# Six groups instead of eight in the first phase of a two-layer network, and register reads queued behind weight loads

## The chip, the core and the metric

The kernel runs on one core of a Trainium2 chip. A core has a matrix engine (TensorE, PE in the profile), a vector engine (VectorE, DVE), an activation engine (ScalarE, ACT), a general engine (GpSimd, POOL) and a queue engine (SyncE, SP), which issues most of the DMAs. Each works through its own instructions in order, and they wait for each other by semaphores. The metric is device time in microseconds, lower is better; the median of three runs is shown.

## The reference

Three blocks follow each other, all in float32.

```python
# attention with rotary embedding: 2 batches, 8 heads, 576 tokens, 64 wide
scores = scale * matmul(rotate(q), rotate(k).T); attn = softmax(scores); x = attn @ v   # -> 1152 tokens x 512
# first network: 512 -> 2048 -> 512
h = x @ w_in
g = maximum(h, 0) + log1p(exp(-abs(h)))          # softplus
x = g @ w_out
# second network: each token with x @ w_skip > 0 goes to the best of 8 experts, 512 -> 1024 -> 512
e_idx = argmax(xc @ w_gate); gate_w = softmax(...)[e_idx]
out[do_compute] = xc + gate_w * (maximum(xc @ w1[e], 0) @ w2[e])
```

`w_in` and `w_out` are scaled so that float32 accuracy is needed; the weights of the first network arrive as 64-bit words.

## The kernel before

Every product of float32 data is made from halves: a tile is split into a high part, which ACT writes, and the rest, which DVE writes, and three matmuls (high by high, low by high, high by low) take the place of one.

**Attention** fills the first 184 us. It ends with `xh` and `xl`, the two halves of its output, in the layout in which the first network reads them.

**First network** (class `Moe1`). The 2048 hidden units are 16 groups `f` of 128. `weights(f)` loads a group's rows of `w_in` and `w_out` through SP (two loads into a staging ring `st` of two buffers) and unpacks them: on DVE three integer instructions (L561 to L563), on ACT a copy (L565), on DVE a subtraction (L566), for each of the two halves. `hidden(ci, f)` multiplies a range `ci` of tokens (L579) and computes softplus with six instructions of ACT and four of DVE per range (twice for a range of two blocks). `out_mm` (L620) adds the group's share to the output tiles, which stay in PSUM. PSUM holds five output tiles beside the rest, so the work goes in phases, `ranges` in the main function: phase 0 takes the first 512 tokens with groups 0 to 7, phase 1 the other 640 tokens with all 16 groups, phases 2 and 3 the first and second 256 of the first 512 tokens with groups 8 to 15. What phase 0 added up is kept in `part` and added again at the end of phases 2 and 3. Groups 8 to 15 therefore stay in SBUF from phase 1 to the end: `ring` says which pool a group's buffer comes from, `ahead` in which step `(phase, f)` it is asked for. The out matmuls of a step are written two steps behind its hidden ones (`pend`, `second`).

**Routing** runs beside phases 2 and 3: as soon as an output tile is ready it is written to `x2d`, transposed and multiplied with the gate (`turned`, `logits`), and `route` works out the place of its tokens. `first_tile` and `fetch(0)` gather the first 128 tokens of expert 0 early. `EARLY` names the steps in which the first five chunks of that expert's weights are loaded (through the same staging ring) and split (`split_w`), `XGT` the step in which the gathered rows are transposed. The last steps and the first tile's hidden matmuls are written in a fixed order (`REST`, `MORE`).

**Second network** (class `Moe2`, method `tiles`). Sorted by expert, the tokens are up to 17 tiles of 128 rows, 9 here. A tile needs eight chunks of weights of 128 x 1024, four of `w1` (part 0) and four of `w2` (part 1), each loaded into its buffer `raw[c]` by SP and split by ACT (L842) and DVE (L846). The expert of tile `T` and whether it differs from the one before are read by SP from the tensor `ei` into registers (`next_w`, L941 and L942); a load whose tile has the expert of the tile before is issued but moves nothing. `nt`, the number of tiles, is read by all engines for the `If` behind the ninth tile (L1220).

**Order.** Except for the part written by hand, a planner sets each engine's order from the order of the program and a simulated timeline of its own: an instruction that it believes ready may be put ahead of others of the same engine. `issue_after(x)` makes what is traced inside it follow `x` on `x`'s engine; it adds no wait.

Of the kernel before, what the change touches and what calls it, by code (L numbers as in the profile page):

```python
# [38 lines left out]
EARLY_RAW = 1  # L39
LATE_W = 4  # L40
HOLD = ((3, 15),)
EARLY = ((2, 11), (2, 12), (2, 13), (3, 10), (3, 12))
XGT = (3, 13)
REST = ((12, 13), (14,))

# [580 lines left out]
class Moe2:  # L626
# [4 lines left out]
    def __init__(self, tc, w_skip, w_gate, w1, w2, cst, x2d, out, rp, sp):  # L631
        self.tc, self.nc = tc, tc.nc
        nc = tc.nc
        self.w1, self.w2, self.cst, self.x2d, self.out, self.rp, self.sp = w1, w2, cst, x2d, out, rp, sp
        self.w9 = rp.tile([128, 4, 9], F32, name="w9")
        nc.scalar.dma_start(self.w9[:, :, 0:8], w_gate.rearrange("(k p) e -> p k e", p=128))
        with nc.allow_non_contiguous_dma(reason="512 words once"):
            nc.scalar.dma_start(self.w9[:, :, 8:9], w_skip.rearrange("(k p o) -> p k o", p=128, o=1))
        self.found_rows, self.late = None, (None, None)
        self.oh = rp.tile([128, 9, 8], BF16, name="oh")  # L640
        self.routed = []
        self.tok = rp.tile([128, 9, 1], F32, name="tok")
        self.xg, self.did = {}, {}
        self.lg = rp.tile([128, 9, 9], F32, name="lg")
        self.m0 = rp.tile([128, 9], F16, name="m0")
        self.extra = None
        self.ohp = sp.tile([128, 9, 128], F16, name="ohp")
        self.at = sp.tile([128, 9, self.ST], F32, name="at")
# [170 lines left out]
    def load_chunk(self, r, e, c, queue=None, **kw):  # L819
        queue = queue or self.nc.sync  # L820
        es = slice(e, e + 1) if isinstance(e, int) else bass.ds(e, 1)
        if c < 4:
            queue.dma_start(r, self.w1[es, 128 * c : 128 * c + 128, :].rearrange("o p n -> p (o n)"), **kw)
        else:
            k = 256 * (c - 4)
            src = self.w2[es, k : k + 256, :].rearrange("o (j p) n -> p (o j) n", p=128)
            queue.dma_start(r.rearrange("p (j n) -> p j n", j=2), src, **kw)

    def load_w(self, e, part, **kw):

        for c in range(4 * part, 4 * part + 4):
            self.load_chunk(self.raw[c], e, c, **kw)

    def split_w(self, T, c, raw=None):
        nc = self.nc
        raw = self.raw[c] if raw is None else raw
        at = c if T == 0 or c > 3 else 4 * (T - 1) + c
        wp, n = self.ring[2 if c > 3 and (T, c) != (0, 4) else 0 if at % 6 < 2 else 1]
        w = wp.tile([128, 2, 2, 512], F32R, name=f"ws{T}{c}", tag="w", bufs=n).rearrange("p x a n -> p x (a n)")
        late = (T, c) in ((0, 5), (0, 6), (0, 7))  # L840
        with self.tc.issue_after(self.ex.ins) if late else nullcontext():
            hi = nc.scalar.copy(w[:, 0], raw)  # L842

        after = {(0, 5): self.found_rows, (0, 6): self.late[1], (0, 7): self.late[1]}.get((T, c))
        with self.tc.issue_after(after) if after else nullcontext():
            self.did[T, c] = hi.ins, nc.vector.tensor_sub(w[:, 1], raw, w[:, 0].bitcast(F32)).ins  # L846
        return w
# [90 lines left out]

    def next_w(self, T):

        e = self.nc.sync.value_load(self.ei[0:1, T : T + 1], min_val=0, max_val=7)  # L941
        new = self.nc.sync.value_load(self.ei[0:1, 24 + T : 25 + T], min_val=0, max_val=1)  # L942
        self.load_w(e, 0, cond=new)
        return e, new

    def tiles(self, Ts, xp, ps_x, ps_y, ps_h, st=None):

        Ts, prev, got = list(Ts), None, []
        if st:
            for c in (5, 6, 7):  # L950
                self.load_chunk(self.raw[c], 0, c)
            with self.tc.issue_after(self.wrote.ins):
                for c in range(EARLY_RAW):
                    self.load_chunk(self.raw[c], 0, c)
            self.early.append(self.split_w(0, 5))
            self.fetch(1, xp)
            st = self.turn(0, st, xp, ps_x)
            self.early += [self.split_w(0, c) for c in (6, 7)]
            with self.tc.issue_after(self.late[0]):
                for c in range(EARLY_RAW, 5):  # L960
                    self.load_chunk(self.raw[c], 0, c, self.nc.scalar)
            Ts.pop(0)
            first = self.result(0, st, xp, ps_y, lambda: got.append(self.gather(1, xp, ps_x)))
            st = got[0]
            nxt = self.next_w(1)
        else:
            first, nxt = None, self.next_w(Ts[0])
            self.fetch(Ts[0], xp)
            st = self.gather(Ts[0], xp, ps_x)
        for T in Ts[1:3]:  # L970
            self.fetch(T, xp)
        for T in Ts:
            cur = nxt
            st = self.hidden(T, st, xp, [ps_h.tile([128, 512], F32, name=f"mh{T}{c}", tag="mh") for c in range(2)])
            with ExitStack() as order:
                if first:


                    order.enter_context(self.tc.issue_after(self.half))
                    for done in self.did[1, 1]:  # L980
                        order.enter_context(self.tc.issue_after(done))
                    first()
                    first = None
                if T + 1 in Ts:
                    nxt = self.next_w(T + 1)
                    following = self.gather(T + 1, xp, ps_x)
            if T + 3 in Ts:
                self.fetch(T + 3, xp)
            st = self.turn(T, st, xp, ps_x)
            if prev:  # L990
                self.result(T - 1, prev, xp, ps_y)()
            self.load_w(cur[0], 1, cond=cur[1])
            prev, st = st, following
        self.result(Ts[-1], prev, xp, ps_y)()
# [65 lines left out]
def attention_moe_moe_kernel(ctx: ExitStack, tc, q, k, v, w_in, w_out, w_skip, w_gate, w1, w2, tab, out):  # L1060
    nc = tc.nc

    def pool(stack, name, bufs=1, space=None, **kw):
        if space is not None:
            kw["space"] = space
        return stack.enter_context(tc.tile_pool(name=name, bufs=bufs, **kw))
# [8 lines left out]
    wa = pool(ctx, "wa")  # L1075

    with ExitStack() as s1:
# [29 lines left out]
        moe2.ring, moe2.early = [(wa, 2), (wc, 4)], []  # L1107
        with ExitStack() as s2:
            gq, gp = pool(s2, "gq"), pool(s2, "gp")
            ring = [(pool(s2, "wb0"), 3), (pool(s2, "wb1"), 2), (wc, 4)]  # L1110
            tp = pool(s2, "tp")
            hp, accp = pool(s2, "hp", 2, PSUM), pool(s2, "accp", 5, PSUM)
            psa = pool(s2, "psa", 1, PSUM)

            part = tp.tile([128, 4, 512], F32, name="part")
            ranges = ((0, 0, 8), (1, 0, 16), (2, 8, 16), (3, 8, 16))
            steps = [(ph, ci, f) for ph, (ci, f0, f1) in enumerate(ranges) for f in range(f0, f1)]
            due, pend, accs = [], [], {}
            ahead = {0: [(0, 2), (1, 3), (2, 4), (3, 5), (4, 6), (5, 7)],
                     1: [(0, 8), (2, 9), (3, 10), (5, 11), (6, 12), (8, 13), (9, 14), (11, 15)], 2: [], 3: []}  # L1120

            def ready(ph, t):
                if ph == 0:
# [27 lines left out]
            for ph, ci, f in steps:  # L1151
                for z, fw in ahead[ph]:
                    if z == f:
                        wb, n = ring[(0, 0, 0, 1, 1, 2, 2, 2, 2)[(fw - 2) % 9]]

                        with ExitStack() as order:
                            for done in att.parted[-2:] if fw >= LATE_W else ():
                                order.enter_context(tc.issue_after(done))
                            moe1.weights(fw, wb, st, n)
# [30 lines left out]
            def rest(t, fs):  # L1190
                for ph, ci, f, g in pend:
                    if f in fs:
                        moe1.out_mm(ci, f, g, accs[ph], 8, 15, t)

            with tc.manual_schedule(engines={nc.tensor.engine}):
                for fs in REST:
# [15 lines left out]
    with ExitStack() as s1:  # L1212

        wp, moe2.rows, wp2, xp, ws = (pool(s1, x) for x in ("wr", "xgp", "wr2", "xp2", "ws"))
        moe2.ring.append((ws, 6))
        moe2.raw = [wp2.tile([128, 1024], F32, name=f"raw{c}") for c in range(5)]
        moe2.raw += [wp.tile([128, 1024], F32, name=f"raw{c}") for c in (5, 6, 7)]
        ps = [pool(s1, "ps_x", 2, PSUM), pool(s1, "ps_y", 2, PSUM), pool(s1, "ps_h", 4, PSUM)]
        moe2.tiles(range(9), xp, *ps, st=st0)
        nt = nc.values_load(moe2.ei[0:1, 20:21], min_val=0, max_val=17)  # L1220
        with tc.If(nt > 9):
            moe2.tiles(range(9, 12), xp, *ps)
            with tc.If(nt > 12):
                moe2.tiles(range(12, 17), xp, *ps)
# [30 lines left out]
```

## Time and profile before

| | |
|---|---|
| median of 3 runs | 546.83 us (546.31 to 548.03) |
| profiled execution | 545.96 us, of which 544.2 us are the span of the profile |
| busy in the span | PE 501.9 us (92%), DVE 438.5 (81%), ACT 387.4 (71%), POOL 192.0 (35%) |
| first network, phase 0 to the tail | 184 to 412.5 us |
| tail of routing, first tiles | 412.5 to 445 us |
| rest of the second network | 445 to 538 us, then the last write and the drain |

Times are microseconds from the start of the span. "busy" counts instructions of an engine, not its waits; matmuls overlap their ends, so the distance from start to start of two of them is what one costs when they follow each other. "idle before" a row is the time in which its engine did nothing, and behind the arrow stands what ended it.

### The profile page before, as it was taken

The numbers are of one execution on the slowest core, as the hardware profiler recorded it, in microseconds if no ns is written. First come the engines' busy times: TensorE is split into PE (matmuls) and PEld (weight loads), VectorE is DVE, ScalarE is ACT, GpSimd is POOL, SyncE is SP. The second block draws the span as 40 slices with busy tenths as digits, with TensorE's granted clock in tenths as the row PEclk, the third lists the DMA queues.
The fourth block names the chain that finished last, engine by engine and source line by source line (L and its number), as shares of the span: only waits on it lengthen the run. The fifth ranks groups of instructions, "written<-read, shape, count | busy, mean of one in ns | idle before, by whom it ended". The sixth has DMA issues, their size and how long they took to land. (4 is left out here: it accounts for less than half of the span.)

```text
span 544.2 us, 9061 instructions
## 1 busy us (share of the span) xinstructions
PE 501.9 (92%) x2900; PEld 422.9 (78%) x2900; DVE 438.5 (81%) x858; ACT 387.4 (71%) x875; POOL 192.0 (35%) x236
## 2 busy tenths in 40 slices
PE   7889988979988999897999999999999979999994
PEld 3677877858767887686999999889987758887773
DVE  6787876898899999989799983454975869888994
ACT  2678987867877785568669884686874468877881
POOL 2868999979864411000000000000200702422331
PEclk9799999998999999999999999999999989999998
DMA  7787365344454023443323330050206604796300
GB/s 200 184 229 210 84 154 136 101 101 116 98 142 140 2 77 102 148 144 112 117 78 117 122 111 1 1 194 1 87 19 231 254 20 124 250 341 219 117 22 34
DMA packets 43014, 67.18 MB, mean 123 GB/s; under 512 B 9824, under 2 KB 24416, under 8 KB 42960
## 3 DMA queue, kind: packets, MB, share of 16 engines
q1 hardware_dynamic: 39184, 59.60, 36.9%
q0 software_dynamic: 1440, 4.20, 2.2%
q10 hardware_dynamic: 2336, 2.74, 1.5%
q8 instruction: 25, 0.41, 0.3%
q14 instruction: 29, 0.24, 0.1%
HBM read 67.30 MB, written 7.15 MB: 137 GB/s over the span
## 5 line engine op out<-in xcount | busy, mean ns | idle before, releaser
L579 PE MATMUL h<-xh,w 128*128 128x320 f32 (+2 forms) x448 | 104.7, 316 | 1.6 <-DVE w L566 1.4
L846 DVE TENSOR_TENSOR ws<-raw,ws 128x1024 fp32r<-128x1024 f32 x67 | 79.3, 1217 | 10.9 <-ACT ws L842 10.5
L620 PE MATMUL acc<-w,gh 128*128 128x512 f32 x288 | 82.5, 396 | 4.8 <-ACT gh L610 4.6
L579 PEld LDWEIGHTS h<-xh,w 128*128 128x128 f32 x448 | 75.3, 188 | 7.3 <-DVE w L566 2.6
L842 ACT CAST ws<-raw 128x1024 fp32r<-128x1024 f32 x67 | 66.7, 1063 | 7.3 <-DMA raw<-in_moe_w_dram 5.5
L579 PE MATMUL h<-xl,w 128*128 128x320 f32 (+2 forms) x224 | 68.1, 313 | 0.0
L684 POOL TENSOR_SCALAR sc<-lg 128x2 f32<-128x2 f32 (+1 forms) x3 | 0.9, 291 | 187.0 <-DVE lg L667 187.0
L620 PEld LDWEIGHTS acc<-w,gh 128*128 128x128 f32 x288 | 52.3, 188 | 16.5 <-ACT gh L610 6.7
L922 PE MATMUL y<-ws,hT 128*128 128x512 f32 x216 | 57.1, 403 | 0.5 <-DVE hT L908 0.2
L262 ACT ACTIVATE P<-s,m 128x576 f32<-128x576 f32 x64 | 48.0, 752 | 10.3 <-DVE m L249 10.0
L249 DVE TENSOR_REDUCE m<-s 128x1 f32<-128x576 f32 x64 | 48.0, 749 | 8.8 <-PE s L241 7.3
L934 POOL DMA_INDIRECT out_dram<-yo,si x9 | 28.0, 3115 | 75.1 <-DVE yo L933 73.2
L332 PE MATMUL t<-ct,P 128*128 128x128 f32 x288 | 47.0, 289 | 7.9 <-DVE pt L327 3.7
L874 PE MATMUL mh<-ws,xgT 128*128 128x512 f32 x192 | 50.4, 408 | 3.9 <-ACT xgT L869 3.0
L410 PE MATMUL pv<-pt,vv 128*128 128x320 f32 (+1 forms) x272 | 49.9, 315 | 3.3 <-DVE x L422 2.6
L620 PE MATMUL acc<-w,gl 128*128 128x512 f32 x144 | 48.4, 392 | 0.2 <-DVE gl L611 0.2
L874 PEld LDWEIGHTS mh<-ws,xgT 128*128 128x128 f32 x192 | 36.0, 193 | 14.0 <-ACT xgT L869 3.4
L922 PEld LDWEIGHTS y<-ws,hT 128*128 128x128 f32 x216 | 39.2, 188 | 9.7 <-DVE ws L846 0.5
L332 PEld LDWEIGHTS t<-ct,P 128*128 128x128 f32 x288 | 35.3, 147 | 14.4 <-DVE pt L327 5.6
L603 DVE SCALAR_TENSOR_TENSOR y<-u,y 128x320 f32<-128x320 f32 (+2 forms) x56 | 27.2, 496 | 23.2 <-ACT u L601 23.1
L410 PEld LDWEIGHTS pv<-pt,vv 128*128 128x128 f32 x272 | 40.3, 194 | 6.6 <-DVE x L422 3.8
L594 ACT ACTIVATE y<-h 128x320 f32<-128x320 f32 (+2 forms) x56 | 25.0, 447 | 27.5 <-PE h L579 26.6
(266 smaller groups left out, 1125.9 us busy)
## 6 DMA issues: line engine op xcount, KB each, us to landing
raw<-in_moe_w_dram SPq DMA_DIRECT2D x68, 512.0 KB
raw<-in_moe_w_in_dram SPq DMA_DIRECT2D x16, 512.0 KB
raw<-in_moe_w_out_dram SPq DMA_DIRECT2D x16, 512.0 KB
ks<-kT SPq DMA_DIRECT2D x32, 144.0 KB
kl<-kT SPq DMA_DIRECT2D x32, 144.0 KB
qs<-qT SPq DMA_DIRECT2D x32, 128.0 KB
wr<-in_moe_w_dram SPq DMA_DIRECT2D x5, 512.0 KB
x2d<-x SPq DMA_DIRECT2D x9, 256.0 KB
```

The source lines that it names most:

```text
L249: self.latest = nc.vector.tensor_reduce(st["m"][:, a : a + 1], st["ps"][a][:, :, 0:288], axis=AX.XY, op=ALU.max, negate=True)
L262: nc.scalar.activation(P[:, 576 * a : 576 * a + 576].rearrange("p (c n) -> p c n", c=2), ps[:, :, 0:288], AF.Exp, bias=m[:, a : a + 1], ac ...
L332: nc.tensor.transpose(ps[:, 128 * i : 128 * i + 128], src, ident)
L410: nc.tensor.matmul(ps[:, 0:n], lhsT=vv[:, j, :], rhs=pt[:, x, self.place(c, i), 0:n], **se)
L579: nc.tensor.matmul(ps[c][:, 0:m], lhsT=w[:, 0, x, 128 * k : 128 * k + 128], rhs=src[:, k, c0 + m * c : c0 + m * c + m], start=z == 0, stop ...
L603: nc.vector.scalar_tensor_tensor(y[:, c], u[:, c], 1.0, y[:, c], op0=ALU.subtract, op1=ALU.subtract)
L620: nc.tensor.matmul(acc[t], lhsT=g[x][:, 128 * j : 128 * j + 128], rhs=w[:, 1, y, :], start=f == f0 and z == 0, stop=f == f1 and z == 2,)
L842: hi = nc.scalar.copy(w[:, 0], raw)
L846: self.did[T, c] = hi.ins, nc.vector.tensor_sub(w[:, 1], raw, w[:, 0].bitcast(F32)).ins
L874: i = mm()
L922: nc.tensor.matmul(py, lhsT=ht[:, x, o : o + 128], rhs=w[:, y, 512 * j : 512 * j + 512], start=c == 0 and j == 0 and z == 0, stop=c == 3 a ...
L934: nc.gpsimd.indirect_dma_start(out=self.out, out_offset=bass.IndirectOffsetOnAxis(ap=si.bitcast(U32), axis=0), in_=yo, in_offset=None, bou ...
```

## The change

Phase 0 takes groups 0 to 5 (`N0 = 6`), phases 2 and 3 take groups 6 to 15, so ten groups stay in SBUF from phase 1 to the end. The buffers for them are found in this way: the list that picks a group's pool is written out, group 14 takes the second place of `wb1` and group 15 one of the two buffers of `wa`, which groups 0 and 1 leave free. Because `wa` then has one buffer for the first expert's chunks and not two, chunk 1 goes to `wc`. `EARLY` moves: the first chunk stays in step (2,11), the others go to (3,9) to (3,12), before (2,12), (2,13), (3,10) and (3,12). `ahead`, the out matmuls' first group and the ranges follow.

In `next_w` the two register reads of a tile now follow, on SP, the last chunk load of part 0 of the tile before (`self.asked`); so does SP's read of `nt`. The first tile's reads have none before them. `load_chunk` and `load_w` return the last load for this.

```diff
-EARLY = ((2, 11), (2, 12), (2, 13), (3, 10), (3, 12))
+EARLY = ((2, 11), (3, 9), (3, 10), (3, 11), (3, 12))
+N0 = 6
...
-        wp, n = self.ring[2 if c > 3 and (T, c) != (0, 4) else 0 if at % 6 < 2 else 1]
+        wp, n = self.ring[2 if c > 3 and (T, c) != (0, 4) else 0 if at % 6 < (2 if T else 1) else 1]
...
     def load_w(self, e, part, **kw):
         for c in range(4 * part, 4 * part + 4):
-            self.load_chunk(self.raw[c], e, c, **kw)
+            last = self.load_chunk(self.raw[c], e, c, **kw)
+        return last
...
     def next_w(self, T):
-        e = self.nc.sync.value_load(self.ei[0:1, T : T + 1], min_val=0, max_val=7)
-        new = self.nc.sync.value_load(self.ei[0:1, 24 + T : 25 + T], min_val=0, max_val=1)
-        self.load_w(e, 0, cond=new)
+        with self.behind():
+            e = self.nc.sync.value_load(self.ei[0:1, T : T + 1], min_val=0, max_val=7)
+            new = self.nc.sync.value_load(self.ei[0:1, 24 + T : 25 + T], min_val=0, max_val=1)
+        self.asked = self.load_w(e, 0, cond=new)
         return e, new
+    def behind(self):
+        return self.tc.issue_after(self.asked.ins) if self.asked else nullcontext()
...
-            ring = [(pool(s2, "wb0"), 3), (pool(s2, "wb1"), 2), (wc, 4)]
+            ring = [(pool(s2, "wb0"), 3), (pool(s2, "wb1"), 2), (wc, 4), (wa, 2)]
...
-            ranges = ((0, 0, 8), (1, 0, 16), (2, 8, 16), (3, 8, 16))
+            ranges = ((0, 0, N0), (1, 0, 16), (2, N0, 16), (3, N0, 16))
...
-            ahead = {0: [(0, 2), (1, 3), (2, 4), (3, 5), (4, 6), (5, 7)],
-                     1: [(0, 8), (2, 9), (3, 10), (5, 11), (6, 12), (8, 13), (9, 14), (11, 15)], 2: [], 3: []}
+            ahead = {0: [(0, 2), (1, 3), (2, 4), (3, 5), (5, 6)],
+                     1: [(0, 7), (2, 8), (3, 9), (5, 10), (6, 11), (8, 12), (9, 13), (11, 14), (12, 15)], 2: [], 3: []}
...
-                        wb, n = ring[(0, 0, 0, 1, 1, 2, 2, 2, 2)[(fw - 2) % 9]]
+                        wb, n = ring[(0, 0, 0, 1, 1, 2, 2, 2, 2, 0, 0, 0, 1, 3)[fw - 2]]
...
-                        moe1.out_mm(ci, f, g, accs[ph], 8, 15, t)
+                        moe1.out_mm(ci, f, g, accs[ph], N0, 15, t)
...
-        nt = nc.values_load(moe2.ei[0:1, 20:21], min_val=0, max_val=17)
+        with moe2.behind():
+            nt = nc.values_load(moe2.ei[0:1, 20:21], min_val=0, max_val=17)
```

## Rows read from the trace of the kernel before

**Rows 1.** Busy us (count) by stage: PE, PEld, DVE, ACT, POOL; then clock, DMA.

```profile
184.00:251.00 67.00, 60.40 (x292) 48.54 (x291) 62.97 (x119) 46.65 (x97) 7.97 (x14) 1.00 0.34 106
251.00:351.60 100.60, 100.60 (x562) 91.41 (x561) 77.42 (x166) 74.17 (x189) 0.00 (x0) 1.00 0.25 82
351.60:412.50 60.90, 60.86 (x421) 54.87 (x421) 40.62 (x127) 42.62 (x116) 4.05 (x9) 1.00 0.27 92
412.50:445.00 32.50, 27.46 (x152) 20.82 (x151) 21.62 (x53) 16.16 (x22) 12.15 (x10) 0.95 0.45 165
445.00:544.20 99.20, 92.08 (x434) 73.11 (x432) 83.74 (x91) 71.69 (x92) 29.45 (x11) 0.98 0.45 152
```

**Rows 2.** The same view, first phase's end and second phase's start.

```profile
218.30:265.00 46.70, 40.77 (x206) 33.80 (x205) 43.16 (x84) 33.36 (x76) 0.00 (x0) 1.00 0.44 134
```

**Rows 3.** Timeline of PE: start, length, instruction, idle before it, what ended that.

```profile
224.45 0.73 PE L579 MATMUL h<-xh,w 128*128 128x512 f32 x2 [1.02 <-DVE w L566]
...
248.06 2.58 PE L620 MATMUL acc<-w,gh 128*128 128x512 f32 x10 [3.18 <-ACT gh L610]
```

**Rows 4.** Timeline of DVE in the second phase.

```profile
253.64 0.68 DVE L563 SCALAR_TENSOR_TENSOR wt<-raw,wt 128x512 uint32<-128x512 uint32 x1
254.24 0.42 DVE L561 TENSOR_SCALAR wt<-raw 128x512 uint32<-128x512 uint32 x1
254.57 0.89 DVE L608 TENSOR_TENSOR r<-r,u 128x320 f32<-128x320 f32 x2
```

**Rows 5.** Timeline of PE, hidden matmuls 512 and 256 columns wide.

```profile
209.60 0.62 PE L579 MATMUL h<-xh,w 128*128 128x512 f32 x2
210.06 0.39 PE L579 MATMUL h<-xl,w 128*128 128x512 f32 x1
...
367.23 0.40 PE L579 MATMUL h<-xh,w 128*128 128x256 f32 x2
367.47 0.28 PE L579 MATMUL h<-xl,w 128*128 128x256 f32 x1
```

**Rows 6.** Groups of ACT by shape: busy us, mean ns, idle before.

```profile
L601 ACT ACTIVATE u<-y 128x512 f32<-128x512 f32 x8 | 5.1, 641 | 0.1
L601 ACT ACTIVATE u<-y 128x256 f32<-128x256 f32 x16 | 6.7, 419 | 0.3
L842 ACT CAST ws<-wr 128x1024 fp32r<-128x1024 f32 x5 | 5.2, 1047 | 1.2 <-PE acc L620 1.0 <-DMA wr<-in_moe_w_dram 0.2
```

**Rows 7.** Timeline of ACT, a late split of the first expert.

```profile
388.67 1.05 ACT L842 CAST ws<-wr 128x1024 fp32r<-128x1024 f32 x1 [0.98 <-PE acc L620]
```

**Rows 8.** Register reads on SP: count, min/median/max ns, first and last start.

```profile
L941 SPq TENSOR_LOAD <-ei x8: 262/270/472, 424.5 to 435.6; - x8
L1220 SPq TENSOR_LOAD <-ei x1: 447/447/447, 436.7 to 436.7; - x1
```

**Rows 9.** Timeline of SP, chunk loads of tiles 1 and 2.

```profile
426.23 5.34 SPq L823 DMA_DIRECT2D raw<-in_moe_w_dram  x4
...
437.82 1.35 SPq L823 DMA_DIRECT2D raw<-in_moe_w_dram  x4
```

**Rows 10.** Timelines of ACT and DVE around tile 2's first split.

```profile
437.89 1.04 ACT L842 CAST ws<-raw 128x1024 fp32r<-128x1024 f32 x1 [5.27 <-DMA raw<-in_moe_w_dram]
...
432.67 2.35 DVE L846 TENSOR_TENSOR ws<-raw,ws 128x1024 fp32r<-128x1024 f32 x2
438.97 1.23 DVE L846 TENSOR_TENSOR ws<-raw,ws 128x1024 fp32r<-128x1024 f32 x1 [3.95 <-ACT ws L842]
```

**Rows 11.** Timeline of PE at tile 2's first hidden matmuls.

```profile
439.48 0.73 PE L874 MATMUL mh<-ws,xgT 128*128 128x512 f32 x2 [2.99 <-ACT xgT L869]
440.85 3.63 PE L874 MATMUL mh<-ws,xgT 128*128 128x512 f32 x8 [0.64 <-DVE xgT L869]
```

**Rows 12.** Busy time right behind that wait, columns as in rows 1.

```profile
440.85:444.28 3.43, 3.43 (x8) 2.55 (x9) 3.10 (x4) 2.39 (x4) 0.00 (x0) 0.53 0.00 0
```

**Rows 13.** Waits of SP: us in total, times, longest.

```profile
SPq L827 <- DVE ws L846: 36.1, 28, 7.2
```

More of the change, by code (lines that the diff above doesn't have):

```diff
@@ L642, in __init__ @@
         self.tok = rp.tile([128, 9, 1], F32, name="tok")
-        self.xg, self.did = {}, {}
+        self.xg, self.did, self.asked = {}, {}, None
         self.lg = rp.tile([128, 9, 9], F32, name="lg")
@@ L822, in load_chunk @@
         if c < 4:
-            queue.dma_start(r, self.w1[es, 128 * c : 128 * c + 128, :].rearrange("o p n -> p (o n)"), **kw)
+            src = self.w1[es, 128 * c : 128 * c + 128, :].rearrange("o p n -> p (o n)")
+            return queue.dma_start(r, src, **kw)
         else:
@@ L826, in load_chunk @@
             src = self.w2[es, k : k + 256, :].rearrange("o (j p) n -> p (o j) n", p=128)
-            queue.dma_start(r.rearrange("p (j n) -> p j n", j=2), src, **kw)
+            return queue.dma_start(r.rearrange("p (j n) -> p j n", j=2), src, **kw)
     def load_w(self, e, part, **kw):
         for c in range(4 * part, 4 * part + 4):
-            self.load_chunk(self.raw[c], e, c, **kw)
+            last = self.load_chunk(self.raw[c], e, c, **kw)
+        return last
     def split_w(self, T, c, raw=None):
@@ L966, in tiles @@
         else:
+            self.asked = None
             first, nxt = None, self.next_w(Ts[0])
```

## The prediction

> **What bounds the kernel now.** I read the clock and the busy time by stage first [rows 1], then TensorE's timeline where a stage shows idle time, then the engines whose names end those waits. The reader is to see in [rows 1] that TensorE (PE) is busy 100.60 of 100.60 us in most of the second phase, 60.86 of 60.90 in the third and fourth, and 92.08 of 99.20 in the last stage, where what is missing is the last result's way out and the drain. Two stretches leave PE idle: 184 to 251 us (6.6 us) and 412.5 to 445 us (5.04 us). The change touches both. Whatever it moves elsewhere is worth something only if it makes PE's own work longer or makes PE wait.
>
> In the first stretch VectorE (DVE) is the bound: from 218.3 to 265 us DVE is busy 43.16 of 46.70 and PE 40.77, so 5.93 us of PE are lost there [rows 2]. The largest are 1.02 us for a weight group (the seventh's hidden matmuls) and 3.18 us for `gh` of the first phase's last out matmuls [rows 3]. In the second stretch PE waits 2.99 and then 0.64 us for the transposed rows of tile 2 [rows 11], because ScalarE (ACT), in order, stands 5.27 us at a chunk of tile 2 [rows 10]. That chunk is not late because data are moved: SyncE (SP) issues tile 1's four chunk loads from 426.23 to 431.57 us and tile 2's first one at 437.82 [rows 9], and between them it reads registers: the pairs of all later tiles, up to 436.2 us, and `nt` at 436.7 [rows 8].
>
> **Part 1: six groups in the first phase.** PE's work stays nearly the same. Two groups leave the first phase with 24 hidden matmuls of 512 columns and come back in phases three and four as 48 of 256 columns; the out matmuls are 12 per group either way. Spacing: 209.60 to 210.06 us for two matmuls of 512, 0.23 each; 367.23 to 367.47 for two of 256, 0.12 each [rows 5]. 24 x 0.23 = 5.52 against 48 x 0.12 = 5.76: **+0.24 us**, bounds 0 and +0.5.
>
> Weight loads of the array double for those groups, 24 more. The Trainium skill (TensorE: Matmul & The Clock Gate, "The mechanism" under Part 3) says that a weight load overlaps a running matmul only where the row group differs, which here it never does; its "LDWEIGHTS" section gives columns / 1.2 ns, and my estimate from that is 24 x 0.107 = 2.6 us more. The 0.12 us spacing of [rows 5], each matmul with its own load, leaves no room for an exposed load, so the measurement decides for +0.24.
>
> What goes: from start to start an instruction of 512 columns takes DVE 0.60 us (253.64 to 254.24), L561 0.33 and one of 320 columns 0.405 [rows 4]. A weight group is two halves of L561 and three of 0.60, 4.3 us; the softplus of a 512-wide step is four of 0.60, 2.4. Per step of the first phase DVE owes 6.7 us, PE only 24 x 0.23 = 5.5: DVE falls behind by over 1 us a step, and the seventh and eighth step pay. After the change PE goes from the sixth group straight to the second phase, whose groups 0 to 5 lie unpacked already; a step there is 24 matmuls of 320 and 15 of 512 columns, 24 x 0.147 (by their share of columns between the two spacings) + 15 x 0.23 = 7.0 us of PE, and two new weight groups are asked for per three steps, so DVE owes (2 x 4.3 + 3 x 8 x 0.405) / 3 = 6.1. DVE is then no longer the slower one. The waits up to the sixth group (6.6 - 5.93 = 0.67 us) stay. Of the 5.93 us in [rows 2] I take 5.2 as gone and leave 0.7, since DVE starts the second phase with some backlog. Bounds: 0, if the backlog only moves (it can't grow, DVE is asked for less in the same time of PE), to 5.93.
>
> What it adds elsewhere: ACT and DVE do the softplus of the moved groups in 256-wide pieces, 0.42 us for 256 columns against 0.64 for 512 [rows 6]: 24 x 0.42 - 12 x 0.64 = +2.4 us on ACT, and two thirds of it on DVE, which has four instructions where ACT has six. PE covers it: ACT is busy 42.62 and DVE 40.62 of 60.90 there [rows 1]. Without that cover it would cost its length.
>
> Chunks 1 to 4 of the first expert now get the buffers of groups 7 to 10, which come free only as the last phase uses those up. So four splits stand in four successive steps (3,9) to (3,12); before, three were done in the second phase. A split is 1.05 us on ACT [rows 6] and waited 0.98 for an out matmul where it came that late [rows 7]. A step is PE's 12 x 0.12 + 6 x 0.23 = 2.8 us; ACT's is six of 0.42, 2.5. With a split it is 3.6, with the wait 4.5. The out matmuls run two to three steps behind the hidden ones, 6 to 8 us, which takes up most of 4 x 0.8 to 4 x 1.7. I take **+0.5 us**; bounds 0 and 6.8. Two of the moved loads wait on SP for a staging buffer, up to a step or two, with the `x2d` rows and gate rows of tiles 0 and 1 behind them; these are asked for by row gathers after the last phase, four and more steps later, so I cost that at nothing.
>
> Sum of part 1: -5.2 + 0.24 + 0.5 = **-4.5 us**.
>
> **Part 2: register reads behind chunk loads.** The pair for tile 1 stays ahead. A read's load is 0.27 us, and eight pairs start from 424.5 to 435.6 with four chunk loads between them [rows 8], so a pair costs SP between 0.54 and 11.1 / 7 = 1.6 us; I take 1.15, as the 6.25 us from 431.57 to 437.82 hold reads alone. Tile 2's first chunk now waits for its own pair behind 431.57: about 432.7 instead of 437.82. The chunks are free as DVE ends tile 1's splits, the last at 432.67 + 2.35 = 435.02 [rows 10]; so the loads are issued between 432.7 and 435.1 instead of 437.82 and 439.2. ACT starts 4.9 us earlier, DVE 3.95, straight after tile 1. ACT's cast of tile 2's rows comes at about 434.6, before PE needs it at 436.5; DVE's half follows one split, 435.02 + 1.15 + 0.6 = 436.8. Of 2.99 + 0.64 = 3.63 us of PE idle I leave 0.7 (DVE's lead over PE shrinks too): **-2.9 us**; bounds 0 and -3.63.
>
> The clock: in 440.85 to 444.28 the granted share is 0.53 [rows 12], the lower level of 1.2 GHz, after a stretch in which PE did two matmuls in 4.4 us; eight matmuls take 3.43 us, 0.43 each against 0.23. Without the gap I expect no fall: 8 x 0.2 = **-1.6 us**; bounds -1.6 and +1.6, should a new gap bring a second one.
>
> What the moved reads delay: 1.15 us on SP per tile, in front of the second half's loads of the tile before. SP waits there for DVE anyway, 36.1 us in 28 waits [rows 13], over 1 us each; without that cover loads would be late by 1.15 us per tile, which PE would feel only as far as splits wait for them. `nt` (0.6 us) moves among the last of these waits.
>
> Sum of part 2: **-4.5 us**. What is late next is DVE, busy 83.74 us of the last stage against PE's 92.08 [rows 1].
>
> **Sum.** -9.0 us on the profiled execution's 545.96 (span 544.2 and 1.76 around it) gives 537.0. The median of the runs shown is 0.87 above that execution: **538 us**. About 0.3% (1.6 us) is what a measurement of this kernel tells from no change.
>
> **Rivals.**
> - The read part gives little (0.14): tile 2's loads move up, but PE's wait only moves to DVE's halves or to `raw` still being read. For: DVE has 9% less work there than PE, no more. Against: 3.95 us of plain DVE idle [rows 10]. With 1 us gained: 546.8 - 4.5 - 1 = 541.3.
> - The phase part gives little (0.12): DVE's backlog meets PE at the first out matmuls of the second phase. For: DVE is busy 92% of the stretch to 265 us. Against: its debt per step falls below PE's. With 1 us gained: 541.3.
> - Neither (0.06), the planner's new order costing elsewhere what it gains: 546.5.
> - Slower (0.10): ACT, in order, waits at each of the four late splits for an out matmul, with the softplus behind it that PE's next out matmul needs. If PE's order leaves no other work between them, a step becomes the whole round, hidden 1.4 + ten softplus instructions 4.2 + split 1.05 + out 1.4 = 8 us instead of 2.8. For: [rows 7] shows the wait. Against: 0.98 there stopped no matmul, with PE busy 60.86 of 60.90. Two such steps cost 10.4 us and bring 546.8 - 9.0 - 0.5 + 10.4 = 547.7, the point from which it decides; four bring 558. I take 549.
>
> **How the numbers follow.** My forecast has 0.58, spread from 535 (all of 5.93, 3.63 and 1.6 gained) to 540. The first two rivals lie at 541 to 543. The range 534.8 to 543.5 leaves out the last two and the edges, some 0.2. Faster by over 0.3%: 0.58 + 0.14 + 0.12 = 0.84; within: 0.06; slower: 0.10.
>
> **What would show it.** Right: PE idle from 218 to 265 us under 1.5; SP's chunk loads of tile 2 a few us behind tile 1's, with one pair of reads between; no granted clock below full from 430 to 450; PE as busy as now in the last two phases. Wrong: PE waits for `gh` of the second phase's first steps; ACT waits for `acc` in (3,9) to (3,12) with PE idle beside it; the 2.99 us wait with another releaser.

## The result and the profile after

After: 542.77 us, the median of 9 runs (541.47 to 544.44); before, on the same chips, 547.37 (545.92 to 549.62). The ratio is 0.9917 (95% interval 0.9896 to 0.9938), a gain of 4.5 us where 9 were forecast. The profiled execution after took 541.82 us, with a span of 540.0.

Two marks on TensorE's timeline part the change. From the first hidden matmul of the first network to its last out matmul, 227.77 us became 227.28. From there to the last matmul of the second network, 125.18 became 123.09. The rest of the difference between the two profiled executions, 1.6 us, lies in attention, which the change does not touch. So in the traces only 2.6 us of gain lie in what was changed. The timed executions of the kernel before that stand beside the experiments had a mean granted clock of 0.976 to 0.986 where they took under 547 us and of 0.965 to 0.978 where they took longer, and the profiled one, at 0.981, is among the shorter.

First the timeline of TensorE in the profile after (start, length, instruction, idle before it and what ended that). These five rows answer to [rows 3] and [rows 11]; the line numbers are two to four higher than before, so that L620 is L622 here and L874 is L878:

```profile
231.21 4.14 PE L622 MATMUL acc<-w,gh 128*128 128x512 f32 x10 [4.02 <-ACT gh L612]
...
406.73 0.73 PE L622 MATMUL acc<-w,gh 128*128 128x512 f32 x2 [1.98 <-ACT gh L612]
...
438.57 3.52 PE L878 MATMUL mh<-ws,xgT 128*128 128x512 f32 x14 [0.51 <-DVE ws L850]
...
466.48 2.53 PE L878 MATMUL mh<-ws,xgT 128*128 128x512 f32 x8 [0.75 <-DVE ws L850]
...
470.01 1.66 PE L926 MATMUL y<-ws,hT 128*128 128x512 f32 x6 [0.54 <-DVE ws L850]
```

The shorter waits of the first phase are gone, 1.02 us among them. The one at its end, 3.18 us in [rows 3], is still there and is 4.02. At the last out matmuls there is a new one of 1.98 us. In place of 2.99 and 0.64 us at tile 2 there are 0.51, and 1.3 us at tile 4. Next, busy time by stretches of the profile after, columns as in [rows 1]; the first row answers to [rows 2], the second, which follows the 4.02 us, to [rows 12], and the third to the same stretch in [rows 1]:

```profile
218.00:265.00 47.00, 42.98 (x233) 38.67 (x232) 43.50 (x90) 36.37 (x89) 0.00 (x0) 0.96 0.36 113
...
231.21:235.04 3.83, 3.83 (x10) 3.02 (x11) 3.83 (x10) 3.31 (x9) 0.00 (x0) 0.55 0.28 101
...
412.50:445.00 32.50, 30.56 (x172) 23.67 (x172) 25.29 (x57) 21.21 (x30) 12.13 (x10) 1.00 0.41 148
```

In the first row TensorE is idle 4.02 us, all of it that one wait, where it was idle 5.93 us in [rows 2]; in the third row 1.94 us where it was 5.04. The reader is also to see the clock: the lower level no longer comes at 441 us, but it now comes at 231.6, behind the longer wait, for 3.4 us in which a matmul of 512 columns takes 0.43 us and not 0.23. That is some 1.5 us of loss, as much as the change took away at 441.

The second part did at its place what was forecast. SyncE's timeline in the profile after, to hold against [rows 9]:

```profile
423.84 9.54 SPq L826 DMA_DIRECT2D raw<-in_moe_w_dram  x8
```

Tile 1's and tile 2's eight chunk loads now lie within 9.5 us, with one pair of reads between. From tile 1's first hidden matmul to tile 2's are 6.0 us and not 9.2; from tile 2's to tile 3's 13.7 and not 15.4, the clock's share. But from tile 4's to tile 5's are 15.7 us where there were 13.4. VectorE's timeline in the profile after shows why:

```profile
434.33 0.69 DVE L873 TENSOR_TENSOR xgT<-xgt,xgT 128x512 fp32r<-128x512 f32 x1
437.18 0.16 DVE L935 TENSOR_TENSOR si<-xg,e 128x1 int32<-128x1 f32 x1 [2.17 <-DMA out_dram<-yo,si]
...
460.90 1.22 DVE L850 TENSOR_TENSOR ws<-raw,ws 128x1024 fp32r<-128x1024 f32 x1
465.10 0.16 DVE L935 TENSOR_TENSOR si<-xg,e 128x1 int32<-128x1 f32 x1 [2.98 <-DMA out_dram<-yo,si]
465.21 1.22 DVE L850 TENSOR_TENSOR ws<-raw,ws 128x1024 fp32r<-128x1024 f32 x1
```

`si`, the row numbers to which a tile's result is scattered, has three buffers, and the planner puts it early. The fourth `si` waits until the first tile's scatter has landed, the fifth until the second's, and the splits behind them wait too. Before, that `si` ran at 440.71, behind the late split of [rows 10], 2.4 us after the scatter had landed at 438.32.

### The profile page after: what moved, and what is told of

Read it like the earlier page. It is cut to its first block, busy times and chain, and to the rows that moved or that the text cites. A ratio compares the mean times of both kernels' runs of the same rounds, so it can differ in the third digit from the quotient of the medians.

```text
span 540.0 us, 9141 instructions
## 1 busy us (share of the span) xinstructions
PE 500.6 (93%) x2924; PEld 423.8 (78%) x2924; DVE 437.7 (81%) x866; ACT 388.1 (72%) x887; POOL 195.8 (36%) x236
## 5 line engine op out<-in xcount | busy, mean ns | idle before, releaser
L622 PE MATMUL acc<-w,gh 128*128 128x512 f32 x288 | 85.0, 401 | 6.1 <-ACT gh L612 6.0
L581 PEld LDWEIGHTS h<-xh,w 128*128 128x128 f32 x464 | 77.8, 188 | 4.2 <-ACT P L264 0.4
L581 PE MATMUL h<-xl,w 128*128 128x320 f32 (+2 forms) x232 | 69.6, 308 | 0.0
L622 PEld LDWEIGHTS acc<-w,gh 128*128 128x128 f32 x288 | 53.4, 192 | 16.9 <-ACT gh L612 6.8
L938 POOL DMA_INDIRECT out_dram<-yo,si x9 | 31.5, 3499 | 69.5 <-DVE yo L937 59.2
L878 PE MATMUL mh<-ws,xgT 128*128 128x512 f32 x192 | 49.0, 399 | 1.7 <-DVE ws L850 1.3
L622 PE MATMUL acc<-w,gl 128*128 128x512 f32 x144 | 49.3, 392 | 0.0
L605 DVE SCALAR_TENSOR_TENSOR y<-u,y 128x320 f32<-128x320 f32 (+2 forms) x58 | 27.3, 484 | 23.0 <-ACT u L603 23.0
L581 PEld LDWEIGHTS h<-xl,w 128*128 128x128 f32 x232 | 43.3, 188 | 2.1
```

Source lines behind the costliest of these rows:

```text
L581: nc.tensor.matmul(ps[c][:, 0:m], lhsT=w[:, 0, x, 128 * k : 128 * k + 128], rhs=src[:, k, c0 + m * c : c0 + m * c + m], start=z == 0, stop ...
L605: nc.vector.scalar_tensor_tensor(y[:, c], u[:, c], 1.0, y[:, c], op0=ALU.subtract, op1=ALU.subtract)
L622: nc.tensor.matmul(acc[t], lhsT=g[x][:, 128 * j : 128 * j + 128], rhs=w[:, 1, y, :], start=f == f0 and z == 0, stop=f == f1 and z == 2,)
L878: i = mm()
L938: nc.gpsimd.indirect_dma_start(out=self.out, out_offset=bass.IndirectOffsetOnAxis(ap=si.bitcast(U32), axis=0), in_=yo, in_offset=None, bou ...
```

## Experiments

Each kernel was timed against the kernel of before the change on the same chip. The timed ratios have intervals of 0.2 to 0.4% to either side, so a difference of 1 or 2 us is read from the profiled executions, by the same two marks (length of the first network, length of the rest).

**1. Register reads alone**: the phases are those of before.

```diff
-N0 = 6
+N0 = 8
```

(with `EARLY`, `ahead` and the pools of before)

> Register reads behind chunk loads alone, phases as before. Theory: the traces of before and after differ in the routing tail and the second network by 3.0 us of TensorE idle gained, 1.6 us of half clock gained, and 1.4 us of new waits (VectorE's si behind the scatter of tile 0, found at 465.10 after): -3.2 us, a ratio of 0.994. The half clock at 441 us is gone and the waits for si on VectorE (2.2 and 3.0 us) are there. Rival: the reads gave everything that was measured (-4.6 us, 0.9917) and the phase part nothing.

Measured: 545.95 us, ratio 0.9942 (0.9914 to 0.9969), -3.2 us. The rest fell from 125.18 to 122.91 us. The tiles are 6.0 and 13.7 us apart as after, the fourth and fifth 15.7: the waits for `si` are there. The first network took 229.41 us, 1.6 more than before with the same instructions; TensorE's timeline and clock at the end of the first phase of this kernel:

```profile
246.86 1.65 PE L622 MATMUL acc<-w,gh 128*128 128x512 f32 x3 [3.37 <-ACT gh L612]
```

```profile
246.86:250.20 3.34, 3.34 (x8) 2.66 (x9) 3.34 (x8) 3.22 (x9) 0.00 (x0) 0.50 0.39 107
```

The same wait as in [rows 3] is here followed by the half clock, which the profiled execution before did not have. That the kernel before can lose these 1.6 us too, and that this is one reason for timed gains larger than the traces', is likely but not shown.

**2. Six groups alone**: `behind()` gives nothing to follow.

```diff
-        return self.tc.issue_after(self.asked.ins) if self.asked else nullcontext()
+        return nullcontext()
```

> Six groups in the first phase alone, reads as before. Theory: from the first hidden matmul to the last out matmul 227.8 us became 227.3, so -0.5 us, a ratio of 0.999; the wait for gh at the end of the first phase is still about 4 us with 3.4 us of half clock behind it, and 2 us are waited at the last out matmuls; the half clock at 441 us is there again. Rival: the profiled execution after is an unlucky one and the phase part brings what the prediction said, -4.5 us, 0.992.

Measured: 544.42 us, 0.9929 (0.9897 to 0.9961), -3.9 us timed, but the first network took 227.25 us against 227.77: in the trace the theory holds. The wait of 3.97 us with its half clock, the 1.98 us and the half clock at 438 are there. The timed interval reaches from -2.1 to -5.6 us, so the rival's 4.5 is not excluded by it; what speaks against it is that the two waits are found again. What the theory did not have: the rest took 123.94 us, 1.2 less than before, with 1.93 us of wait at tile 2 in place of 2.99 and no wait for `si`. So the two parts do not add in the traces: the reads are worth 2.3 us beside eight groups (experiment 1) and 0.9 beside six (123.94 to 123.09).

**3. Nine buffers for `si`.**

```diff
-        si = xp.tile([128, 1], I32, name=f"si{T}", tag="si", bufs=3)
+        si = xp.tile([128, 1], I32, name=f"si{T}", tag="si", bufs=9)
```

> After, with nine buffers for si and not three, so that no si has to wait for a scatter to land. Theory: VectorE's 2.2 us at 437 and 3.0 us at 465 go, and with them TensorE's 0.5 and 1.4 us behind them: 541 us against after's 542.8. Rival: TensorE is then held by the splits of the same tiles anyway (VectorE is the busier engine there), nothing changes: 542.8.

Measured: 542.19 us, 0.9880 (0.9844 to 0.9915). The rest took 121.36 us against 123.09 after, 1.7 us less. Tile 4 to tile 5 is back at 13.4 us. Not all came: without the wait for a buffer the planner puts five `si` in a row, and two of them wait for gathered rows. VectorE's timeline of this kernel:

```profile
433.95 0.29 DVE L935 TENSOR_TENSOR si<-xg,e 128x1 int32<-128x1 f32 x3
435.21 0.16 DVE L935 TENSOR_TENSOR si<-xg,e 128x1 int32<-128x1 f32 x1 [0.97 <-DMA xg<-x2d,gi]
435.79 0.16 DVE L935 TENSOR_TENSOR si<-xg,e 128x1 int32<-128x1 f32 x1 [0.42 <-DMA xg<-x2d,gi]
```

TensorE then waited 1.08 us for a split at 437.15, and tile 2 came 7.4 us behind tile 1 and not 6.0. The theory is right on what the wait is and a little high on its price.

**4. Later groups asked for later.**

```diff
-            ahead = {0: [..., (5, 6)],
-                     1: [(0, 7), (2, 8), (3, 9), (5, 10), (6, 11), ...
+            ahead = {0: [...],
+                     1: [(1, 6), (2, 7), (4, 8), (5, 9), (7, 10), (8, 11), ...
```

> After, with groups 6 to 10 asked for two to three steps later. Theory: the wait of 4.0 us at the end of the first phase stays because VectorE unpacks groups 6 and 7 (ready at 225.2 and 236.3, first used at 263.4 and 270.4) between the softplus of the last step of 512; without them there the wait falls under 1 us and no half clock follows: -4.0 - 1.7, some 537 us. Rival: the 12 us from the last 512-wide hidden matmul to its gh are the length of the softplus chain itself on two engines beside 320-wide steps; the wait stays over 3 us and the time at 542 to 543.

Measured: 543.61 us, 0.9909 (0.9874 to 0.9945), wait 3.82 us: a miss, though it does not speak for the rival either. The edit asks for groups 6 to 11 two steps later and for 12 and 13 one step later, but VectorE's order around the wait was that of after; group 6 was unpacked at 227.5 us, which is after's 225.2 and the 2.3 us by which this execution came later out of attention. As these timelines read, the planner pulls the unpacking forward wherever VectorE looks free, whatever the step in which it is written. So this kernel does not test the theory.

**5. Unpacking behind the softplus**: the step of experiment 4, and an order that the planner has to keep.

```diff
+                            if fw >= N0:
+                                order.enter_context(tc.issue_after(did[-2]))
                             moe1.weights(fw, wb, st, n)
...
                     pend.append((ph, ci, f, moe1.hidden(ci, f, hp, gp, gq)))
+                    did.append(moe1.last)
```

(`last` is the softplus's last instruction on VectorE)

> After, with the unpacking of a group from 6 on written behind the softplus of the step two before on VectorE (asking later alone moved no instruction, since a planner places them). Theory: the 4.0 us wait at the end of the first phase is VectorE's order: 4.3 us of unpacking that nobody needs for 35 us stand in front of the softplus of the last 512-wide step. Behind it, gh comes some 4 to 5 us earlier, the wait falls under 0.5 us and the half clock behind it goes: 4.0 + 1.7 less, 537 us. Rival: the latency is ACT's, which runs two steps' softplus in turn; the wait stays above 2.5 us, 541 to 543.

Measured: 538.48 us, 0.9836 (0.9799 to 0.9874). The first network took 223.09 us, 4.2 less than after. The wait and its half clock are gone; the half clock came once more at 402.7, behind the 1.99 us at the last out matmuls, which is why not all of 5.7 us shows. VectorE's timeline after, and then of this kernel, from the last 512-wide hidden matmul (ended 219.2 and 220.5 us) to its `gl`:

```profile
222.04 0.69 DVE L568 TENSOR_TENSOR w<-wt,w 128x512 fp32r<-128x512 f32 x1 [0.37 <-ACT w L567]
224.15 0.43 DVE L563 TENSOR_SCALAR wt<-raw 128x512 uint32<-128x512 uint32 x1 [1.42 <-DMA raw<-in_moe_w_in_dram]
224.50 0.68 DVE L568 TENSOR_TENSOR w<-wt,w 128x512 fp32r<-128x512 f32 x1
225.10 0.69 DVE L564 SCALAR_TENSOR_TENSOR wt<-raw,wt 128x512 uint32<-128x512 uint32 x1
225.70 1.09 DVE L605 SCALAR_TENSOR_TENSOR y<-u,y 128x512 f32<-128x512 f32 x2
226.87 0.43 DVE L563 TENSOR_SCALAR wt<-raw 128x512 uint32<-128x512 uint32 x1
227.21 0.69 DVE L565 SCALAR_TENSOR_TENSOR wt<-raw,wt 128x512 uint32<-128x512 uint32 x1
227.82 0.69 DVE L608 TENSOR_TENSOR r<-r,y 128x512 f32<-128x512 f32 x1
...
229.22 0.68 DVE L564 SCALAR_TENSOR_TENSOR wt<-raw,wt 128x512 uint32<-128x512 uint32 x1
229.82 0.69 DVE L610 TENSOR_TENSOR r<-r,u 128x512 f32<-128x512 f32 x1
...
232.77 0.68 DVE L613 TENSOR_TENSOR gl<-r,gh 128x512 fp32r<-128x512 f32 x1
```

```profile
219.24 0.69 DVE L613 TENSOR_TENSOR gl<-r,gh 128x512 fp32r<-128x512 f32 x1 [0.69 <-ACT gh L612]
223.69 1.09 DVE L605 SCALAR_TENSOR_TENSOR y<-u,y 128x512 f32<-128x512 f32 x2 [3.76 <-ACT u L603]
224.70 1.09 DVE L608 TENSOR_TENSOR r<-r,y 128x512 f32<-128x512 f32 x2
225.70 1.09 DVE L610 TENSOR_TENSOR r<-r,u 128x512 f32<-128x512 f32 x2
227.73 0.69 DVE L613 TENSOR_TENSOR gl<-r,gh 128x512 fp32r<-128x512 f32 x1 [0.94 <-ACT gh L612]
228.34 0.76 DVE L563 TENSOR_SCALAR wt<-raw 128x512 uint32<-128x512 uint32 x2
```

After, the softplus (L605, L608, L610, L613) has unpacking before and between all its steps, and even a wait of 1.42 us for a weight load that nothing urgent needed; `gh` ended 12.0 us behind the hidden matmul. Here it ended 7.2 us behind it, although VectorE stands idle for 5.4 us. The engine was not short of time; it did its work in the wrong order. The edit moves ScalarE's share of the unpacking as well: after, two of its copies (L567, at 221.37 and 222.25, 0.64 us each) stood among the softplus's instructions, and here the next copy runs at 233.37. ScalarE still runs two steps' softplus in turn, and the wait is gone: the rival falls. How the 4.8 us by which `gh` ends earlier divide between the two engines is not shown.

**6. Splits one step earlier**: groups 6 to 9 in the pool that the chunks take.

```diff
-EARLY = ((2, 11), (3, 9), (3, 10), (3, 11), (3, 12))
+EARLY = ((2, 11), (3, 8), (3, 9), (3, 10), (3, 11))
...
-                        wb, n = ring[(0, 0, 0, 1, 1, 2, 2, 2, 2, 0, 0, 0, 1, 3)[fw - 2]]
+                        wb, n = ring[(0, 0, 0, 1, 2, 2, 2, 2, 1, 0, 0, 0, 1, 3)[fw - 2]]
```

> After, with groups 6 to 9 in the pool whose buffers the first expert's chunks take (10 in the pool of 6), so that the four late splits come one step earlier, (3,8) to (3,11). Theory: the 1.98 us at the last out matmuls come from four splits of 1.05 us on ACT in four steps in a row, the softplus of the last step behind them; a step more between the last split and the end takes 1 to 2 us off that wait: 541 to 542 us. Rival: the wait is the length of the last step's softplus beside the gathered rows' cast, whatever the splits do: 2 us stay, 542.8.

Measured: 541.63 us, 0.9892 (0.9851 to 0.9933); the first network 225.55 us, 1.7 less than after. TensorE's timeline of this kernel at the last out matmuls:

```profile
404.69 0.73 PE L622 MATMUL acc<-w,gh 128*128 128x512 f32 x2 [0.26 <-ACT gh L612]
```

The wait fell from 1.98 to 0.26 us, as the theory has it. On ACT the four splits still wait for out matmuls or loads (0.44 and 1.09 us before two of them), but now there is a step to make up for it. In this trace the rest took 121.39 us, as with nine buffers for `si`, though there are three here: the fourth `si` waited 1.04 us and the fifth not at all, and the second tile's scatter kept GpSimd busy for 1.7 us and not for 7.4 as after. In the other four traces with three buffers and the reads behind (after, experiments 1, 4 and 5) both waits are there at 2.2 and 2.8 to 3.1 us. So their price is not the same in every trace.

**7. The three edits together** (3, 5 and 6; experiment 9 is the same kernel again).

> All three edits in one kernel: nine buffers for si, unpacking behind the softplus, splits one step earlier. Theory: what they take away lies in three places that don't touch each other, so it adds: -1.9, -5.7 and -1 to -2 us, 533 to 535. Rival: TensorE finds the next wait behind each, half of it is left: 537 to 539.

> The kernel with all three edits (nine buffers for si, unpacking behind the softplus, splits one step earlier) once more, on the chip of the next two kernels, as what they are compared with: 533 to 536 us again.

Measured: 534.46 us, 0.9778 (0.9738 to 0.9819), and again 536.14, 0.9783 (0.9760 to 0.9807): the first in the theory's range, the second just above it. The first network took 219.85 and 219.96 us, the rest 121.39 and 121.45. By the ratios this kernel is 12 us faster than before and some 7.5 us faster than after. Its row for the stretch of [rows 2], busy time as there:

```profile
216.00:265.00 49.00, 49.00 (x276) 44.67 (x275) 41.80 (x89) 38.73 (x98) 0.00 (x0) 1.00 0.30 98
```

TensorE is busy 49.00 of 49.00 us. VectorE, busy 43.16 of 46.70 before and 43.50 of 47.00 after, is busy 41.80 of 49.00.

**8. Eight groups, with the reads part, nine buffers and the order of 5.**

```diff
-N0 = 6
+N0 = 8
...
-            ahead = {..., 1: [(0, 8), (2, 9), (3, 10), (5, 11), ...
+            ahead = {..., 1: [(1, 8), (3, 9), (4, 10), (6, 11), ...
```

(with `EARLY` and the pools of before)

> Eight groups in the first phase as before, register reads behind chunk loads, nine buffers for si, and the unpacking of groups 8 on behind the softplus. Theory: with VectorE's order put right the end of the first phase costs nothing with eight groups either, and what six groups save is only the 2.2 us that groups 6 and 7 make TensorE wait in the first phase, against 2 us at the late splits: within 1 us of the kernel with six groups and the first two edits, 535 to 537. Rival: with eight groups VectorE owes over 1 us a step by then, the wait at the end of the phase stays over 2 us: 539 to 541.

Measured: 538.95 us, 0.9848 (0.9808 to 0.9888). The first network took 223.41 us, against 227.77 and 229.41 with the planner's order: the wait at the end of the phase is gone with eight groups as well. What stays are 0.36, 1.02, 0.77 and 0.26 us in the first phase. So order alone, with eight groups kept, gives 4.4 us or more there. The time is 2 us above what was expected of it; 0.8 us of that lies in the rest (122.21 us, with a wait of 2.18 us for a split of tile 1), the other part is not placed.

**10. The kernel of 7 with the register reads in front**, the edit of experiment 2.

> The kernel with all three edits, but the register reads in front again as before the change. Theory: with VectorE's wait for the scatter out of the way the reads part is worth what the prediction gave it, 2.9 us of idle and 1.6 us of half clock: 4 to 5 us slower than with the reads behind, 538 to 539.5. Rival: what the reads part gives is only the 2 us by which the stretch behind the last out matmul became shorter after: 536.5.

Measured: 535.76 us, 0.9789 (0.9759 to 0.9820), in timing not to be told from the 536.14 beside it. In the trace the rest took 123.17 us against 121.45, 1.7 us longer: nearer the rival's 2 us than the theory's 4 to 5. No half clock followed here. TensorE's timeline of this kernel at tiles 1 and 2:

```profile
426.59 2.11 PE L878 MATMUL mh<-ws,xgT 128*128 128x512 f32 x8 [1.23 <-DVE ws L850]
429.75 0.73 PE L878 MATMUL mh<-ws,xgT 128*128 128x512 f32 x2 [1.06 <-ACT xgT L873]
431.13 1.19 PE L878 MATMUL mh<-ws,xgT 128*128 128x512 f32 x4 [0.64 <-DVE xgT L873]
```

**11. The kernel of 7 with seven groups.**

```diff
-N0 = 6
+N0 = 7
```

(with `ahead`, the pools and `EARLY` to match)

> The kernel with all three edits, with seven groups in the first phase and not six (three late splits, chunk 1 in the second step of the third phase as before). Theory: group 6 is back in the first phase and its unpacking is the one on which TensorE waited 1.0 us before, with 0.8 to 1.0 us at the out matmuls behind it; the late splits cost nothing any more, so fewer of them save nothing: 1.5 to 2.5 us slower than six groups, 536 to 537. Rival: with VectorE's order put right the number of groups makes no difference: within 0.7 us of six groups.

Measured: 536.01 us, 0.9783 (0.9763 to 0.9802), the same as six groups; the first network 220.32 us against 219.96. The rival holds between six and seven; eight, in experiment 8, cost 3.5 us in the trace of the first network.

## Why the prediction was right in sign and half in size

**The step that failed is "of the 5.93 us in [rows 2] I take 5.2 as gone".** Of this idle time 1.9 us went and 4.02 stayed, where the prediction's own sign was under 1.5. The step was argued from amounts: VectorE owes 6.7 us a step in the first phase and TensorE 5.5, and afterwards 6.1 against 7.0, so it would catch up. For the six shorter waits this held, and they are gone; with eight groups and the order set by hand (experiment 8) four of them remain. But the wait at the end of the phase, more than half of the idle time, did not come from an amount: it goes with six groups and with eight once the order is set (experiments 5 and 8). In the timelines of before and after, the next group's unpacking stands wherever VectorE was free. After, group 6 is ready at 225.2 us (the L568 of 224.50 in the rows of experiment 5) and first multiplied at 263.43; before, group 8 was ready at 242.2 and used at 292.6. VectorE's timeline before, where group 8's unpacking (up to L566) stands in front of the first softplus step of the last 512-wide range:

```profile
240.45 0.43 DVE L561 TENSOR_SCALAR wt<-raw 128x512 uint32<-128x512 uint32 x1 [1.26 <-DMA raw<-in_moe_w_in_dram]
240.91 0.69 DVE L562 SCALAR_TENSOR_TENSOR wt<-raw,wt 128x512 uint32<-128x512 uint32 x1
241.52 0.68 DVE L566 TENSOR_TENSOR w<-wt,w 128x512 fp32r<-128x512 f32 x1
242.12 0.69 DVE L603 SCALAR_TENSOR_TENSOR y<-u,y 128x512 f32<-128x512 f32 x1
```

And TensorE's timeline after, the first use of group 6:

```profile
263.43 0.30 PE L581 MATMUL h<-xh,w 128*128 128x320 f32 x1
```

Asking VectorE for less only let it start the next group sooner; from the last 512-wide hidden matmul to its `gh` there were 12.5 us before and 12.0 after. So the last 512-wide step met the same kind of order in both kernels: 3.18 us of wait with eight groups, 4.02 with six, none with either once the order was set by hand. That the wait "can't grow" was wrong too. The prediction had this case as the low bound, "if the backlog only moves", and close to it as the rival at 541.3 with 0.12; it counted VectorE's busy share of 92% for that rival and let the debt per step decide against it.

**The late splits, +0.5 forecast with bounds of 0 and 6.8, cost 1.98 us.** The mechanism, four splits in a row on ACT with the softplus behind them, was the one described, and the size was too low: ACT waited 0.30 and 0.52 us for out matmuls and 0.35 for a load in front of three of the splits, beside 1.05 us for each split, and the 6 to 8 us by which out matmuls run behind took up less of it than was taken. Experiment 6 shows that one step of slack was missing.

**The clock was put into part 2 alone.** Part 1's longer wait brought a half clock of its own, some 1.5 us. Counted by the distance of matmul starts over their usual spacing (some 0.17 us more than the idle column for each wait), the seven waits from 217 to 248 us before make 7.5 us and the one at 231 after 4.2: 3.3 us went. The last out matmuls' 2.1, the clock's 1.5 and the matmuls' 0.24 came: +0.5, where -0.5 was measured; 1 us is not placed.

**The matmuls' +0.24 held.** The 48 matmuls of 256 columns that take the place of 24 of 512 cost 0.12 us each from start to start, as in [rows 5] (the median is 0.118 before and after). No weight load showed up between them. So the 2.6 us that the prediction estimated from the Trainium skill's rule (TensorE: Matmul & The Clock Gate, "The mechanism" under Part 3) did not come; the prediction took only one half of that rule, which also lets a load for the background weight buffer run ahead of running matmuls.

**Part 2 was right at its place.** Forecast were -2.9 us of wait and -1.6 of clock, and the rest became 2.1 us shorter; tile 1 to 2 became 3.2 us shorter, tile 2 to 3 1.7. Two of its signs came: one pair of reads between the chunk loads, and a full clock from 430 to 450 us. What it missed was 2.3 us between tiles 4 and 5. The prediction asked what the reads are moved past on SP, and left VectorE's own next wait at "DVE's lead over PE shrinks too". An engine that runs 4 us earlier meets what has not become earlier: the scatters of tiles 0 and 1, issued only behind their results. In the kernel of experiment 7 the reads part is worth only 1.7 us in the trace: TensorE waits 1.2 us for a split of tile 1 there with the reads behind or in front, and no half clock follows. Whether that wait covers part of the late loads stays open.

## What to carry to other kernels

A busy share says how much an engine does, not what stands in front of the instruction that somebody waits for: before costing a debt, list that engine's instructions between the cause and the late result, and ask for each when its own result is first used. Where a planner orders the work, changing the place where something is asked for may change nothing; an order has to be stated. And where a stall is taken away, the engine behind it arrives earlier at its next wait, so look up what that one needs, buffers of small tiles included.

## What the runs showed of the hardware

Between 180 and 530 us of the span the granted clock fell to its lower level, 1.2 GHz, ten times in the traces of this case, for 3.4 us each. Six of these falls came at the end of or right behind a wait of TensorE of 3.37 to 4.31 us (after, experiments 1 to 4 and 6), and no wait of that length was without one. One came behind the 2.99 us of [rows 11] and the 0.64 that follow them, two behind waits of 1.93 and 1.99 us (experiments 2 and 5). None came behind the 3.18 us of [rows 3], nor behind five waits of 1.96 to 2.18 us. One came in experiment 6 at 412 us, with no wait of over 0.3 us between it and the fall at 231 us, among the transposes and the narrow matmuls of the routing. Here is that kernel's row, columns as in [rows 1]:

```profile
411.00:416.00 5.00, 5.00 (x37) 3.87 (x37) 1.84 (x13) 2.87 (x4) 0.80 (x4) 0.66 0.43 116
```

A scatter of the same size took 5.3 us from its start on GpSimd to its landing for tile 0 after (431.72 to 437.06), and 11.8 us for tile 1 (453.26 to 465.01). Before, the latter took 6.9 us (459.52 to 466.41). In experiments 1, 4 and 5 it took 11.6 to 11.8 us as well, in experiments 2 and 3 6.9 and 7.3. What makes it longer stays open.
